# A gated block of linear attention and a bilinear feed-forward layer: the output projection of the attention done by seven half-size products

## The chip, the cores and the metric

The kernel runs on one core of one Trainium2 chip. The metric is the device time of one execution in microseconds (us), taken as the median of several runs. A profile is one more execution, with a trace of every engine: TensorE (PE; its weight loads are listed as PEld), VectorE (DVE), ScalarE (ACT), GpSimd (POOL) and SyncE (SP), which here only issues DMAs.

## What is computed

There are S = 2048 tokens of D = 512 features, H = 32 heads of 16, F = 1792 hidden features, all in float32:

```python
g = sigmoid((x * gate_w).sum(-1, keepdims=True))
# a: linear attention
q, k, v = split(x @ wqkv)                            # 32 heads of 16
phi = lambda t: where(t > 0, t + 1, exp(t)) + 1e-6
kv  = einsum("bhsd,bhse->bhde", phi(k), v)
z   = einsum("bhsd->bhd", phi(k))
o   = einsum("bhqd,bhde->bhqe", phi(q), kv) / (einsum("bhqd,bhd->bhq", phi(q), z)[..., None] + 1e-6)
a   = o @ wo
# b: bilinear feed-forward
b   = ((x @ w_gate) * (x @ w_up)) @ w_down
out = g * a + (1 - g) * b
```

The kernel folds kv and wo into one 512 x 512 matrix W' (each head's 16 x 16 block of kv times its 16 rows of wo). What it calls o is then phi(q) divided by its denominator, and a = o @ W'.

## The kernel before

**Precision.** Every float32 operand is split into a high and a low part that TensorE takes as fp32r (`split`: ACT or DVE copies the high part, DVE subtracts it). `mm3` makes one product of three matmuls: high x high, the stationary operand's high part x low, low x high. Nearly all matmuls have 512 columns.

**Phase 1** computes k = x @ wk tile by tile (PSUM tile `pk`), phi(k) and the sums `gt` = phi(k)^T x, and the gate: `gcol` holds g, `ocol` holds 1 - g, one column per tile of 128 tokens.

**Phase 2** goes over two pairs (halves of 1024 tokens) of 16 units each, so units 0 to 31. A unit makes 1024 tokens x 256 columns of two products at once by the 2x2 scheme (Strassen and Winograd): `product(i, ...)` is one of seven products of six matmuls, with the factors of the weights (`wch`, `wcl`, out of `wr`) and of x (`xa`, `xb`, `xc1`, `xc4`, `xc6`, high and low). The products go in the order 2, 3, 4, 1, 5, 6, 7 into the PSUM banks Y, X, R, S (`bY` and so on); ACT copies (`m`, `cross`) and DVE sums (`bR`, `t`, `bS`) between them put the result together. 14 units of a pair are feed-forward units ("f", one block of 128 hidden features), whose two results are multiplied into a hidden tile (`cross`, split to `hh`, `hl`). Two are query units ("q", one group of 16 heads, which is two blocks of 128 features); before, they stand behind the feed-forward blocks 5 and 9, at units 6, 11, 22 and 27.

**The order is written out by hand.** Every engine's list keeps the order of the program. Within a unit there are named places, in this sequence:

```
product 2, high, product 3, low, e, down(0), product 4, m, c, down(1), d,
product 1, t, product 5, down(2), s, down(3), product 6, r, product 7, end
```

`later(n, place, fn)` puts work at a place of unit n. `down(k)` takes the next k tiles off a list `jobs`; the table `shares` says how many at each of a unit's four `down` places. A job of two feed-forward blocks is one PSUM tile `pdn` of 128 tokens x 512 features, six matmuls; then ACT (the first time) or DVE adds it, scaled by `ocol`, to the accumulator `acc` of these tokens in SBUF.

**W'** is made early in phase 2: `kv_unit` (`pkv`), `kv_split` (DVE masks it to blocks of heads with `bmask` as `kvm`; `kvmh`, `kvml` are its parts), `wp_unit(b)` for b = 0 to 3 (PSUM tile `pw`, three matmuls, at places (3, e), (3, d), (4, e), (4, d)), split and parked in DRAM (`wpark`).

**Attention** (`attention`): `quad` makes phi(q) on ACT and DVE (`ex`, `phq`) as the query unit's results come; four `z_part` on ACT and loads through DRAM (`terms`, `zt`) make the denominators in the next two units; `recip` inverts them, `norm` loads them spread out (`rb`), `norm_high` and `norm_low` make o and split it into hidden tiles; `weights` loads W' back; `last` puts eight jobs for this group on the list `jobs`, six matmuls each, scaled by `gcol`. So o @ W' is done per group of heads, and the two groups meet in `acc`.

**Queues.** SyncE issues loads and stores in program order (`dma`), GpSimd issues the accumulating DMAs (`dma_add`) and the output of the first pair. Factors of the weights and of x are also summed by such DMAs: `w_load` loads three blocks, `w_add` adds five; `cb_load`, `x_add`, `cb_split` do it for the second pair's x, which `reload` brings back at the end of the first pair. The hidden tiles have NH = 5 buffers, `acc` has 8 of one tile.

**The end.** Behind the last product 7 come `down(2)`, `low1` (DVE makes the low half of the last hidden tile's second half), `down(1)`, `low0` and what is left of `jobs`.

Of the kernel before, what the change touches and what calls it, by code (L numbers as in the profile page):

```python
# [7 lines left out]
F32 = mybir.dt.float32  # L8
# [6 lines left out]
P = 128  # L15
S = 2048
D = 512
# [13 lines left out]
HB = 8  # L31
NH = 5

# [5 lines left out]

SLOT = {3: 0, 4: 1, 2: 2, 5: 3, 1: 4, 6: 5, 7: 6}  # L40


@with_exitstack
def gated_mix(ctx: ExitStack, tc, xt, xp, x, wqkv, wq, wq_add, wo, wgu, wgu_add, wdn, gate_w, out):
# [75 lines left out]
    zpark = dram.tile([KT * KT, P, P // KT], F32, name="zpark")  # L120
    wpark = [[dram.tile([P, D], F32, name=f"wpark{b}{v}") for v in "hl"] for b in range(KT)]


    order = []
    for f in range(NF):
        order.append(("f", f))
        if f in (5, 9):
            order.append(("q", f // 9))
    units = len(order)
    order = [(pair, *u) for pair in range(NPAIR) for u in order]  # L130

# [49 lines left out]
    with tc.tile_pool(name="p1", bufs=2, reuse_waits="tile") as p1:  # L181
# [168 lines left out]
        pin(nc.vector.reciprocal(gcol, gcol))  # L350
        pin(nc.vector.tensor_scalar(ocol, gcol, -1.0, 1.0, op0=ALU.mult, op1=ALU.add))


# [9 lines left out]
    def do(n, place):  # L363
        for fn in at.pop((n, place), []):
            fn()

    def down(k):
        for fn in jobs[:k]:
            fn()
        del jobs[:k]  # L370

    shares = {2: (0, 1, 1, 1), 6: (1, 0, 1, 0), 7: (1, 0, 1, 0), 10: (1, 1, 1, 2), 11: (1, 2, 1, 2),
              12: (1, 1, 1, 2), 15: (1, 1, 1, 2)}
    early = {units: (2, 4, 2, 2), units + 1: (2, 2, 1, 1)}

    def share(n):
        return early.get(n) or shares.get(n % units, (1, 1, 1, 1))  # L380

# [101 lines left out]
    def down_tiles():  # L483
        return [p2.tile([P, D], F32R, tag=f"d{v}", name=f"d{v}", bufs=NH + 1) for v in "hl"]


    att = {}

    def wp_load():
        att["wv"] = [p2.tile([P, D], F32, tag="acc", name="wv", bufs=8) for _ in range(KT)]  # L490
        att["wo"] = [p2.tile([P, D], F32, tag="ph", name="wo_sb", bufs=4) for _ in range(KT)]
        for k in range(KT):
            dma(att["wv"][k], wqkv[k * P:(k + 1) * P, 2 * D:3 * D])
        for k in range(KT):
            dma(att["wo"][k], wo[k * P:(k + 1) * P, :])

    def g_evac():
        att["g"] = [p2.tile([P, D], F32, tag="acc", name="gts", bufs=8) for _ in range(KT)]
# [48 lines left out]
    def wo_split(b):  # L547
        if b % 2 == 0:
            att.setdefault("woh", []).append(hidden())
        split(*[v[:, b % 2] for v in att["woh"][b // 2]], att["wo"][b])  # L550
# [13 lines left out]
    banks = ["dn", "dn"]  # L564
    left = {(p, i): NF // 2 + 1 for p in range(NPAIR) for i in range(TPP)}

    def down_jobs(pair, group, col):

        def job(i):
            t = pair * TPP + i  # L570
            c, sl = divmod(i, CH // P)
            sl = slice(sl * P, (sl + 1) * P)
            s = col[:, t:t + 1]
            first = (pair, i) not in acc
            if first:
                acc[pair, i] = p2.tile([P, D], F32, tag="acc", name="acc", bufs=8)
            else:
                left[pair, i] -= 1
            ends = not left[pair, i]

            step = D // 2 if ends and pair and i == TPP // 2 - 1 else D
            for o in range(0, D, step):
                cols = slice(o, o + step)
                banks.reverse()
                pd = psum.tile([P, D], F32, tag=banks[0], name="pdn", bufs=2)[:, 0:step]
                for j, ((hh, hl), w2) in enumerate(group() if callable(group) else group):
                    mm3(pd, (hh[:, c, sl], hl[:, c, sl]), [v[:, cols] for v in w2], j == 0, j == 1)
                a = acc[pair, i][:, cols]
# [8 lines left out]
        return [lambda i=i: job((i + TPP // 2) % TPP) for i in range(TPP)]  # L597


    def attention(pair, j, n):  # L600
        phs, group, wrow = {}, {}, {}
        den = {}
        turns = n + 5 == units

        terms = dram.tile([KT, 4 * HB, DH, P], F32, name=f"terms{pair}{j}")
        there = dram.tile([4 * HB, KT, P], F32, name=f"den{pair}{j}")

# [8 lines left out]
        def z_part(i):  # L616
            r, c = parts[i]
            b = 2 * j + r
            z = p2.tile([P, CH], F32, tag="z", name="zq", bufs=4)
            act(z, phs[r, c], AF.Identity, scale=zcol[:, b:b + 1], bias=ezcol[:, b:b + 1])  # L620
            dma(terms[:, HB * i:HB * (i + 1)].rearrange("c h e t -> (h e) c t"), z.rearrange("p (c t) -> p c t", c=KT))

        def z_load(e):

            den[e] = p2.tile([P, KT, P], F32, tag="z", name="zt", bufs=4)
            dma(den[e], terms[:, :, e * KT:(e + 1) * KT].rearrange("c h e t -> (c h) e t"))

# [8 lines left out]

        def recip():
            d = den["d"]
            pin(nc.vector.reciprocal(d, d))
            dma(there.rearrange("h c t -> c h t"), d)  # L640

        def norm(i):
            r, c = parts[i]
            if r not in group:
                group[r] = hidden()
            rb = p2.tile([P, CH], F32, tag="z", name="rb", bufs=4)
            one = there[HB * i:HB * (i + 1)].rearrange("h c t -> h (c t)")
            dma(rb, one[:, None, :].to_broadcast([HB, DH, CH]))
            den[i] = rb

        def norm_high(i):
# [4 lines left out]
        def norm_low(i):  # L656
            r, c = parts[i]
            hh, hl = group[r]
            tt(hl[:, c], den[i], hh[:, c].bitcast(F32), ALU.subtract)

        def weights():
            for r in range(2):
                wrow[r] = down_tiles()
                for src, part in zip(wpark[2 * j + r], wrow[r]):
                    dma(part.bitcast(F32), src)

        def last():

            where = len(jobs) if turns else 0
            jobs[where:where] = down_jobs(pair, lambda: [(group[r], wrow[r]) for r in range(2)], gcol)  # L670

# [8 lines left out]
        for i in range(4):  # L680
            later(n + 3, "e", lambda i=i: norm(i))
        for i, places in enumerate((((n + 3, "s"), (n + 3, "r")), ((n + 3, "end"), (n + 4, "e")),
                                    ((n + 4, "c"), (n + 4, "d")), ((n + 4, "t"), (n + 4, "s")))):
            for fn, (m, place) in zip((norm_high, norm_low), places):
                later(m, place, lambda i=i, fn=fn: fn(i))
        later(*((n + 5, "e") if turns else (n + 3, "c")), weights)
        later(n + 4, "end", last)
        return quad


# [22 lines left out]
    g_evac()  # L713
    for b, (n, place) in enumerate(((1, "e"), (1, "e"), (2, "d"), (2, "s"))):
        later(n, place, lambda b=b: wo_split(b))
    later(0, "s", kv_zeros)
    later(1, "c", kv_unit)
    later(2, "c", z_there)
    later(5, "c", z_sums)
    later(2, "e", kv_split)  # L720
    for b, (n, place) in enumerate(((3, "e"), (3, "d"), (4, "e"), (4, "d"))):
        later(n, place, lambda b=b: wp_unit(b))
    for n, (i, k) in enumerate((i, k) for i in (2, 3, 4, 1, 6, 7) for k in range(2)):
        later(n, "s", lambda i=i, k=k: cb_load(i, k))
# [17 lines left out]
    for n, (pair, kind, m) in enumerate(order):  # L742
        entry = {}
        if n == 6:

            banks[0] = "att"
# [10 lines left out]
        if kind == "f":  # L757
            if half is None:
                half = (hid, entry["d"])
            else:  # L760
                jobs += down_jobs(pair, (half, (hid, entry["d"])), ocol)
                half = None
# [57 lines left out]
```

## Time and profile before

| what | us |
|---|---|
| median of 3 runs | 603.16 (603.09 to 603.17) |
| the profiled execution | 603.08 |
| its span, first to last instruction | 601.4 |
| TensorE busy | 596.5 (99%) |
| DVE busy | 441.9 (73%) |
| ACT busy | 309.2 (51%) |
| POOL busy | 47.1 (8%) |

The granted TensorE clock is 1.000 in this execution. A row of a timeline or chain reads: start in us, duration, engine, operation or line, output <- inputs, partitions x elements, count, and in brackets the idle time ahead of it with what ended it. The duration of a matmul in these rows reaches into the next one's, since matmuls are pipelined; the distance between two starts is what one takes in a row of them.

### The profile page before, as it was taken

The page shows a single profiled execution, that of the slowest core. Times are in us where ns is not written, and L with a number is a line of the kernel's source. Part 1 is how long each engine was busy: PE and PEld are TensorE (multiplying, and loading weights), DVE is VectorE, ACT ScalarE, POOL GpSimd, SP SyncE. Part 2 cuts the span into 40 slices and gives each one's busy share as a digit, 9 for nine tenths or more (in the row PEclk, how much of TensorE's full clock was granted, in tenths as well). Part 3 has the DMA queues.
Part 4 walks back from the last instruction along what each step waited for, and adds up shares of the span by engine and source line. Part 5 has one row for each costly group of instructions (what it writes and reads, how often), then busy time and mean ns, then how long its engine had stood idle before and what let it go on. Part 6 is the DMA issues. An engine that isn't in the chain of part 4 may idle for free.

```text
span 601.4 us, 7610 instructions
## 1 busy us (share of the span) xinstructions
PE 596.5 (99%) x2682; PEld 492.1 (82%) x2682; DVE 441.9 (73%) x693; ACT 309.2 (51%) x534; POOL 47.1 (8%) x63
## 2 busy tenths in 40 slices
PE   9999999999999999999999999999999999999997
PEld 6888888888888888888888888888888888888886
DVE  6977896776787689666888866456677986668864
ACT  3855765586449545373444534654474454643300
POOL 0011100000111110100000020010000000000000
PEclk9999999999999999999999999999999999999999
DMA  8577948667868969658479535334386563553303
GB/s 291 182 195 136 288 94 276 153 189 193 219 175 203 275 156 269 135 126 209 105 223 350 155 138 134 89 87 90 70 192 171 150 168 67 130 146 81 102 1 141
DMA packets 51046, 98.54 MB, mean 164 GB/s; under 512 B 6576, under 2 KB 17584, under 8 KB 50992
## 3 DMA queue, kind: packets, MB, share of 16 engines
q1 hardware_dynamic: 43312, 69.22, 34.1%
q0 software_dynamic: 7408, 28.32, 26.1%
q10 hardware_dynamic: 288, 0.52, 0.3%
q8 instruction: 21, 0.34, 0.2%
q14 instruction: 17, 0.14, 0.1%
HBM read 82.31 MB, written 16.25 MB: 164 GB/s over the span
## 4 chain that ended last, share of the span: by engine, by line
PE 99%; DVE 0%; issue 0%
PE pdn L52 33%; PE bR L52 15%; PE bY L52 14%; PE bX L52 14%; PE pk L52 7%; PE bS L52 7%; PE gt L52 7%; PE warm L52 1%; PE pw L52 0%; PE pkv L52 0%; DVE acc L64 0%; DVE xc1h L108 0%
## 5 line engine op out<-in xcount | busy, mean ns | idle before, releaser
L52 PE MATMUL pdn<-dl,hh 128*128 128x512 f32 x290 | 112.4, 388 | 0.0
L52 PE MATMUL pdn<-dh,hl 128*128 128x512 f32 x290 | 112.4, 388 | 0.0
L52 PE MATMUL pdn<-dh,hh 128*128 128x512 f32 x290 | 112.4, 388 | 0.0
L64 DVE SCALAR_TENSOR_TENSOR acc<-pdn,ocol,acc 128x512 f32<-128x512 f32 (+1 forms) x97 | 71.2, 742 | 30.2 <-PE pdn L52 30.0
L58 ACT ACTIVATE hh<-cross 128x512 fp32r<-128x512 f32 x56 | 35.2, 628 | 89.6 <-DVE cross L61 89.6
L61 DVE TENSOR_TENSOR wcl<-wr,wch 128x512 fp32r<-128x512 f32 (+1 forms) x96 | 73.2, 771 | 0.0
L52 PEld LDWEIGHTS pdn<-dh,hh 128*128 128x128 f32 x290 | 54.5, 188 | 11.2
L52 PEld LDWEIGHTS pdn<-dl,hh 128*128 128x128 f32 x290 | 54.5, 188 | 11.2
L52 PEld LDWEIGHTS pdn<-dh,hl 128*128 128x128 f32 x290 | 54.5, 188 | 11.1
L58 ACT ACTIVATE wch<-wr 128x512 fp32r<-128x512 f32 (+1 forms) x96 | 60.1, 694 | 0.0
L52 PE MATMUL bX<-xbh,wch 128*128 128x512 f32 x128 | 49.8, 389 | 0.0
L52 PE MATMUL bX<-xbl,wch 128*128 128x512 f32 x128 | 49.8, 389 | 0.0
L52 PE MATMUL bX<-xbh,wcl 128*128 128x512 f32 x128 | 49.8, 389 | 0.0
L61 DVE TENSOR_TENSOR bR<-bX,m 128x512 f32<-128x512 f32 x32 | 22.3, 696 | 36.6 <-PE bX L52 31.7
L85 POOL DMA_DIRECT2D wr<-in_wgu_add x28 | 24.3, 868 | 309.5 <-ACT wr L58 175.2
L58 ACT ACTIVATE cross<-bY 128x512 f32<-128x512 f32 x32 | 19.1, 598 | 50.6 <-PE bY L52 50.2
L61 DVE TENSOR_TENSOR t<-bR,cross 128x512 f32<-128x512 f32 x32 | 22.1, 690 | 24.9 <-PE bR L52 11.5
L61 DVE TENSOR_TENSOR hl<-cross,hh 128x512 fp32r<-128x512 f32 x56 | 38.2, 683 | 0.8
L58 ACT ACTIVATE wr<-wr 128x512 f32<-128x512 f32 x64 | 36.5, 620 | 1.2 <-DMA wr<-in_wgu 1.2
L64 DVE SCALAR_TENSOR_TENSOR acc<-pdn,gcol,acc 128x512 f32<-128x512 f32 x32 | 23.7, 749 | 17.5 <-PE pdn L52 17.4
L58 ACT ACTIVATE cross<-bX 128x512 f32<-128x512 f32 x32 | 19.1, 597 | 32.8 <-DVE bS L61 32.6
L58 ACT ACTIVATE m<-bY 128x512 f32<-128x512 f32 x32 | 19.1, 597 | 22.4 <-PE bY L52 22.2
(158 smaller groups left out, 1256.6 us busy)
## 6 DMA issues: line engine op xcount, KB each, us to landing
wr<-in_wgu_add POOLq DMA_DIRECT2D x28, 640.0 KB, 6.3
wr<-in_wgu SPq DMA_DIRECT2D x28, 384.0 KB
wdr<-in_wdn SPq DMA_DIRECT2D x28, 256.0 KB
xraw<-in_x SPq DMA_DIRECT2D x16, 256.0 KB
terms<-zq SPq DMA_DIRECT2D x16, 256.0 KB
zt<-terms SPq DMA_DIRECT2D x16, 256.0 KB
rb<-den SPq DMA_DIRECT2D x16, 256.0 KB
xtraw<-in_xt SPq DMA_DIRECT2D x12, 256.0 KB
```

Source lines behind the costliest of these rows:

```text
L52: tc.keep_in_program_order(nc.tensor.matmul(*args, **kw))
L58: pin(nc.scalar.activation(dst, src, func, **kw))
L61: pin(nc.vector.tensor_tensor(dst, a, b, op=op))
L64: pin(nc.vector.scalar_tensor_tensor(dst, a, scalar, b, op0=op0, op1=op1))
L85: tc.keep_in_program_order(nc.gpsimd.dma_start(dst, src, accum_op=ALU.add))
```

## The change

o @ W' is now one product per pair over both groups of heads: o has 2 x 2 blocks (groups of heads by chunks of 512 tokens), W' has 2 x 2 blocks (halves of the 512 output features by groups of heads), and seven products of their sums replace eight block products.

- The gate g is multiplied into o: the column goes through DRAM (`gpark`) into the tile that held the mask, and `recip` multiplies the inverse by it. The store of the column stands right behind phase 1, ahead of phase 2's loads on SyncE.
- `norm_end` writes each block of o to DRAM (`opark`), and two negated ones.
- `wp_unit` now stands at (2, c), (2, d), (3, e), (3, c); ACT copies W' out, halves go to DRAM (`wraw`), `wp_minus` negates two blocks. From unit 4 on, `ow_load`, `ow_add`, `ow_split` sum and split the seven factors of W', one per unit.
- `o_products` adds 14 jobs per pair (seven products by halves of 512 tokens): in steps (four to a unit, at e, c, t, end) the factor of o is loaded, a step pair later summed by accumulating DMA, a step pair later split (`ready`) and put on a list of its own; `down` takes such a job behind its tiles. A job is 12 matmuls of 256 columns into the PSUM tile `po`, and one or two DVE sums of 512 elements per partition into `acc`. Two of the products go on in the bank of the one before. In all there are 336 such matmuls. The units with these jobs are 12 to 16 and 27 to 31.
- The query units stand behind blocks 2 and 5 in the first pair, behind 1 and 4 in the second: units 3, 7, 18 and 22. NH is 4, `acc` is 4 buffers of two tiles, and the table `shares` changes: unit 16 has (1, 1, 1, 2) instead of (2, 4, 2, 2), unit 17 has (1, 1, 1, 1) instead of (2, 2, 1, 1). `z_there`, `z_sums` and the second bank for down tiles (unit 4 instead of 6) come earlier.

```diff
-NH = 5
+NH = 4
+HALF = D // 2
+OPROD = (
+    (1, ("11", "22"), ("11", "22"), False, (("11", 1),)),
+    (6, ("-11", "21"), ("11", "12"), True, (("22", 1),)),
+    (5, ("11", "12"), ("-22",), False, (("12", -1),)),
+    (7, ("-22", "12"), ("21", "22"), True, (("11", 1),)),
+    (2, ("21", "22"), ("11",), False, (("21", 1), ("22", -1))),
+    (4, ("22",), ("-11", "21"), False, (("11", 1), ("21", 1))),
+    (3, ("11",), ("-22", "12"), False, (("12", 1), ("22", 1))),
+)
+STEPS = ("e", "c", "t", "end")
...
+    for pair, after in enumerate(((2, 5), (1, 4))):
+        for f in range(NF):
+            order.append((pair, "f", f))
+            if f in after:
+                order.append((pair, "q", after.index(f)))
...
+        dma(gpark.rearrange("t p -> p t"), gcol)
...
     def down(k):
         for fn in jobs[:k]:
             fn()
         del jobs[:k]
+        while ojobs and ojobs[0][0] < passed[0]:
+            ojobs.pop(0)[1]()
+        passed[0] += 1
...
-    shares = {2: (0, 1, 1, 1), 6: (1, 0, 1, 0), 7: (1, 0, 1, 0), 10: (1, 1, 1, 2), 11: (1, 2, 1, 2),
-              12: (1, 1, 1, 2), 15: (1, 1, 1, 2)}
-    early = {units: (2, 4, 2, 2), units + 1: (2, 2, 1, 1)}
+    shares = {2: (0, 1, 1, 1), 3: (1, 0, 1, 0), 4: (1, 0, 1, 0), 7: (1, 1, 0, 1), 8: (1, 1, 0, 1), 9: (1, 0, 1, 0)}
+    shares.update({units: (1, 1, 1, 2), units + 1: (1, 1, 1, 1)})
+    shares.update({units + m: v for m, v in ((2, (0, 1, 1, 1)), (3, (1, 0, 1, 0)), (4, (1, 0, 1, 0)),
+                                             (5, (1, 1, 0, 1)), (6, (1, 1, 0, 1)), (7, (1, 0, 1, 0)),
+                                             (15, (1, 1, 0, 1)))})
...
     def wp_unit(b):
+        j, r = divmod(b, 2)
         pw = psum.tile([P, D], F32, tag="att", name="pw", bufs=2)
-        mm3(pw, [v[:, b] for v in att["kvm"]], [v[:, b % 2] for v in att["woh"][b // 2]], True, True)
-        d = down_tiles()
-        split(*d, pw)
-        for there, part in zip(wpark[b], d):
+        mm3(pw, [v[:, b] for v in att["kvm"]], att.pop(("woh", b)), True, True)
+        att["w", b] = w = p2.tile([P, D], F32, tag="ph", name="wrow", bufs=4)
+        act(w, pw)
+        for m in range(2):
+            dma(wraw[f"{m + 1}{j + 1}"][:, r], w[:, m * HALF:(m + 1) * HALF])
+    def ow_split(p):
+        hi, lo = ws.pop(p)
+        act(hi, lo.bitcast(F32))
+        tt(lo, lo.bitcast(F32), hi.bitcast(F32), ALU.subtract)
+        for there, part in zip(wpark[p], (hi, lo)):
             dma(there, part.bitcast(F32))
...
         def recip():
             d = den["d"]
             pin(nc.vector.reciprocal(d, d))
-            dma(there.rearrange("h c t -> c h t"), d)
+            tt(d, d, bmask, ALU.mult)
+            for c in range(2):
+                dma(there[c].rearrange("h c t -> c h t"), d[c * P // 2:(c + 1) * P // 2])
...
+        def norm_end(i):
+            r, c = parts[i]
             stt(den[i], phs[r, c], EPS, den[i], ALU.add, ALU.mult)
-            act(group[r][0][:, c], den[i])
+            o_there(f"{j + 1}{c + 1}", r, den[i])
+            if j == c:
+                act(phs[r, c], den[i], scale=-1.0)
+                o_there(f"-{j + 1}{c + 1}", r, phs[r, c])
...
+    def o_products(pair, step0):
+        def ready(k, place):
+            tiles[k] = o_tiles()
+            split(*tiles[k], raw.pop(k).rearrange("p r t -> p (r t)"))
+            ojobs.append((passed[0] - (place == "end"), lambda: job(k)))
+        def job(k):
+            p, h = divmod(k, 2)
+            _, _, _, goes_on, sums = OPROD[p]
+            ot = [v.rearrange("p (r t) -> p r t", r=2) for v in tiles.pop(k)]
+            w2 = [v.rearrange("p (r c) -> p r c", r=2) for v in wt[p]]
+            if not goes_on:
+                banks.reverse()
+                bank[h] = psum.tile([P, 2, HALF], F32, tag=banks[0], name="po", bufs=2)
+            for s in range(2):
+                for r in range(2):
+                    mm3(bank[h][:, s], [v[:, r, s * P:(s + 1) * P] for v in ot], [v[:, r] for v in w2],
+                        not goes_on and s == r == 0, s == r == 1, True)
+            for block, sign in sums:
+                m, c = int(block[0]) - 1, int(block[1]) - 1
+                a = acc[pair, 2 * c + h][:, :, m * HALF:(m + 1) * HALF]
+                tt(a, a, bank[h], ALU.add if sign > 0 else ALU.subtract)
...
+    for b, (n, place) in enumerate(((2, "c"), (2, "d"), (3, "e"), (3, "c"))):
         later(n, place, lambda b=b: wp_unit(b))
...
-        if n == 6:
+        if n == 4:
             banks[0] = "att"
```

More of the change, by code (lines that the diff above doesn't have):

```diff
@@ L120, in gated_mix @@
     zpark = dram.tile([KT * KT, P, P // KT], F32, name="zpark")
-    wpark = [[dram.tile([P, D], F32, name=f"wpark{b}{v}") for v in "hl"] for b in range(KT)]
+    wraw = {b: dram.tile([P, 2, HALF], F32, name=f"wraw{b}") for b in ("11", "12", "21", "22", "-11", "-22")}
+    wpark = [[dram.tile([P, D], F32, name=f"wpark{i}{v}") for v in "hl"] for i in range(len(OPROD))]
+    gpark = dram.tile([NT, P], F32, name="gpark")
     order = []
[L125 to L130, printed above, removed]
+    for pair, after in enumerate(((2, 5), (1, 4))):
[3 more added lines that the diff above has]
+                order.append((pair, "q", after.index(f)))
+    units = len(order) // NPAIR
     raws, wcs = {}, {}
@@ L497, in g_evac @@
     def g_evac():
-        att["g"] = [p2.tile([P, D], F32, tag="acc", name="gts", bufs=8) for _ in range(KT)]
+        att["g"] = two_by_two("gts")
         for d in range(KT):
@@ L564, in gated_mix, with down_jobs @@
     banks = ["dn", "dn"]
-    left = {(p, i): NF // 2 + 1 for p in range(NPAIR) for i in range(TPP)}
-    def down_jobs(pair, group, col):
+    left = {(p, i): NF // 2 for p in range(NPAIR) for i in range(TPP)}
+    oleft = [2 * len(OPROD) for _ in range(NPAIR)]
+    def down_jobs(pair, group):
         def job(i):
@@ L572, in job @@
             sl = slice(sl * P, (sl + 1) * P)
[L573 to L578, printed above, removed]
+            s = ocol[:, t:t + 1]
+            if (pair, i // 2) not in acc:
+                acc[pair, i // 2] = p2.tile([P, 2, D], F32, tag="acc", name="acc", bufs=4)
+            first = left[pair, i] == NF // 2
+            left[pair, i] -= 1
             ends = not left[pair, i]
+            assert not ends or not oleft[pair]
             step = D // 2 if ends and pair and i == TPP // 2 - 1 else D
@@ L597, in down_jobs @@
         return [lambda i=i: job((i + TPP // 2) % TPP) for i in range(TPP)]
+    opark = {(p, b): dram.tile([2, P, 2, HALF], F32, name=f"opark{p}{b}") for p in range(NPAIR)
+             for b in ("11", "12", "21", "22", "-11", "-22")}
     def attention(pair, j, n):
[L601 to L606, printed above, removed]
+        phs, den = {}, {}
+        terms = dram.tile([2, KT, 2 * HB, DH, P], F32, name=f"terms{pair}{j}")
+        there = dram.tile([2, 2 * HB, KT, P], F32, name=f"den{pair}{j}")
         def quad(r, c, q):
@@ L681, in attention @@
             later(n + 3, "e", lambda i=i: norm(i))
[L682 to L687, printed above, removed]
-        return quad
+        for i, (m, place) in enumerate(((n + 3, "s"), (n + 3, "r"), (n + 3, "end"), (n + 4, "e"))):
+            later(m, place, lambda i=i: norm_end(i))
@@ L760, in gated_mix @@
             else:
-                jobs += down_jobs(pair, (half, (hid, entry["d"])), ocol)
+                jobs += down_jobs(pair, (half, (hid, entry["d"])))
                 half = None
```

106 lines of the change are left out of this document (75 added, 31 removed).

## The prediction

> **What bounds the kernel now.** I read the page first (busy time by engine, granted clock, the chain that ended last), then TensorE's timeline at the end of the run, then the chain in time around each place that the change touches. From the page of the kernel before:
>
> ```profile
> span 601.4 us, 7610 instructions
> ...
> PE 596.5 (99%) x2682; PEld 492.1 (82%) x2682; DVE 441.9 (73%) x693; ACT 309.2 (51%) x534; POOL 47.1 (8%) x63
> ...
> PEclk9999999999999999999999999999999999999999
> ...
> PE 99%; DVE 0%; issue 0%
> ```
>
> TensorE is busy for 99% of the span, at full clock in every slice, and the chain that ends last is TensorE's own list. So the time is the sum of its matmuls. A matmul less is worth its full spacing, and any new idle time of TensorE is paid in full. The other engines have room on average only, so each place where their order changes is looked at by itself. The profiled execution took 603.08 us, 1.68 more than its span; it lies 0.08 under the median of 603.16, so a difference added to either says the same. The three runs lie within 0.08, and I take 0.2% (1.2 us) as what a measurement tells from no change: "same" is 601.95 to 604.37.
>
> **1. The matmuls.** What o @ W' cost per group of heads was 8 tiles of 6 matmuls with 512 columns; two groups, two pairs: 192 matmuls. After, each pair has 14 jobs of 12 matmuls with 256 columns, together 336. The kernel before has both sizes back to back in its last tiles (columns: start, us, engine, line, operation):
>
> ```profile
> 587.66 0.39 PE L52 MATMUL pdn<-dl,hh 128*128 128x512 f32 x1
> ...
> 596.05 0.39 PE L52 MATMUL pdn<-dh,hl 128*128 128x512 f32 x1
> 596.28 0.28 PE L52 MATMUL pdn<-dh,hh 128*128 128x256 f32 x1
> 596.39 0.28 PE L52 MATMUL pdn<-dl,hh 128*128 128x256 f32 x1
> ...
> 597.59 0.28 PE L52 MATMUL pdn<-dh,hl 128*128 128x256 f32 x1
> ```
>
> The durations (0.39, 0.28) overlap, so I go by starts. From 587.66 to 596.05 there are 37 steps: 0.2267 us each. From 596.39 to 597.59 there are 10: 0.120 each. 192 x 0.2267 = 43.5 goes, 336 x 0.120 = 40.3 comes: **-3.2 us**. Seven products in place of eight should give an eighth, 5.4; the small matmul costs more than half of the large one (0.113), and that takes 2.2 back. The ends for this term are 0.110 (596.28 to 596.39) and 0.127 (0.120 plus the 0.007 by which it exceeds half): -6.5 to -0.8. I take 0.120, ten intervals in a row of the same kind.
>
> What of weight loads? Each matmul has one, and the profile shows the last ones thus:
>
> ```profile
> 597.35 0.19 PEld L52 LDWEIGHTS pdn<-dl,hh 128*128 128x128 f32 x1
> 597.47 0.19 PEld L52 LDWEIGHTS pdn<-dh,hl 128*128 128x128 f32 x1
> ```
>
> They start 0.12 apart too, and each lasts longer (0.19) than the matmul's own spacing, so they run under other matmuls. The Trainium skill ("TensorE: Matmul & The Clock Gate", The mechanism) says that a weight load overlaps matmuls in flight only where their row groups differ, which full 128-row tiles don't. By that rule load and matmul would add up; the 0.120 spacing in this trace contradicts it.
>
> **2. Unit 2: W' before its mask is ready.** Before, the first block of W' stood in unit 3, at 129.95 us. After, it stands in unit 2 right behind product 4, ahead of a down-projection tile. Its stationary operand is the masked k-v matrix. Chain in time, then DVE and ACT, before:
>
> ```profile
> 117.71 1.36 PE pdn L52 x6
> 129.95 0.68 PE pw L52 x3
> 118.26 0.85 DVE L61 TENSOR_TENSOR kvm<-pkv,bmask 64x256 f32<-64x256 f32 x2
> 119.21 0.63 ACT L58 ACTIVATE kvmh<-kvm 128x512 fp32r<-128x512 f32 x1 [2.49 <-DVE kvm L61]
> 119.87 0.69 DVE L61 TENSOR_TENSOR kvml<-kvm,kvmh 128x512 fp32r<-128x512 f32 x1 [0.76 <-ACT kvmh L58]
> ```
>
> Product 4 ends at 117.71, where the tile begins; there TensorE now wants the matrix. Its high part is ready at 119.84, its low part at 120.56. DVE's and ACT's lists up to there are unchanged. The first two of the three matmuls of a block use the high part, the third the low part. The high part alone costs 119.84 - 117.71 = 2.1 and up to a weight load (0.19) more; the third matmul, due at 117.71 + 0.45, can start at 120.56 to 120.75: 2.4 to 2.6. With some room for the hand-over of a semaphore 2.2 to 2.8, I take **+2.5**. Nothing can fill this hole, since TensorE's list is fixed; the tile that covered it comes behind.
>
> **3. Unit 16, the start of the second pair.** Before, four tiles stood between product 4 and product 1; after, one.
>
> ```profile
> 332.60 5.44 PE pdn L52 x24
> 338.04 1.36 PE bR L52 x6
> 332.70 0.60 ACT L58 ACTIVATE cross<-bY 128x512 f32<-128x512 f32 x1 [3.80 <-PE bY L52]
> 333.19 1.05 ACT L58 ACTIVATE xc1h<-xc1l 128x1024 fp32r<-128x1024 f32 x1
> 334.27 1.22 DVE L61 TENSOR_TENSOR xc1l<-xc1l,xc1h 128x1024 fp32r<-128x1024 f32 x1 [2.24 <-ACT xc1h L58]
> ```
>
> ACT makes the operand of product 1 only after copying product 4 out, and DVE ends its low part at 335.49. Product 1 used to start at 338.04, 2.5 later. With one tile of 1.36 it could start at 333.96 and needs the low part a matmul later, 334.19: about 1.3 missing, plus a weight load: **+1.35**, bounds 1.0 and 1.6.
>
> **4. The tail.** Before, attention tiles lay behind the last product 7 and gave DVE time for the low half of the last hidden block. After, they are gone, and two tiles are left.
>
> ```profile
> 576.04 21.84 PE pdn L52 x102
> 578.80 0.75 DVE L64 SCALAR_TENSOR_TENSOR acc<-pdn,gcol,acc 128x512 f32<-128x512 f32 x1 [0.61 <-PE pdn L52]
> 579.46 0.68 DVE L61 TENSOR_TENSOR hl<-cross,hh 128x512 fp32r<-128x512 f32 x1
> ```
>
> The low half is ready at 580.14. The sixth matmul of the third tile needs it at 576.04 + 2 x 1.36 + 5 x 0.2267 = 579.89; with the load **+0.45** (0.2 to 0.6).
>
> **5. Units 3 and 4: queries earlier.** The first group of heads moves from unit 6 to unit 3, where ACT also copies two blocks of W' and negates quarters of them, and the first sums start. Around the old place:
>
> ```profile
> 188.19 0.62 ACT L58 ACTIVATE phq<-bS 128x512 f32<-128x512 f32 x1
> 193.01 0.62 ACT L58 ACTIVATE cross<-bY 128x512 f32<-128x512 f32 x1
> 193.97 0.69 DVE L61 TENSOR_TENSOR t<-bR,cross 128x512 f32<-128x512 f32 x1 [1.51 <-ACT cross L58]
> 196.60 1.36 PE bR L52 x6
> L58 ACT ACTIVATE dh<-pw 128x512 fp32r<-128x512 f32 x4 | 2.4, 600 | 1.3 <-PE pw L52 0.9 <-ACT dh L58 0.4
> ```
>
> ACT is behind after the query unit; that delays the copy of product 4 and so `t`, which ends at 194.66, 1.94 ahead of product 6. Two copies of W' add 1.2, with the negations (an estimate: half of 0.6 each, for half the columns, and a fixed part) about 2.2. Against 1.94 that is 0 to 1.0 lost; I take **+0.3**, as most of the copies fall early in unit 3.
>
> **6. What I cost at nothing, and its cover.** VectorE in the units with o products:
>
> ```profile
> L64 DVE SCALAR_TENSOR_TENSOR acc<-pdn,ocol,acc 128x512 f32<-128x512 f32 x95 | 70.3, 747 | 30.0 <-PE pdn L52 29.8
> L61 DVE TENSOR_TENSOR bR<-bX,m 128x512 f32<-128x512 f32 x32 | 22.3, 696 | 36.6 <-PE bX L52 31.7 <-ACT m L58 4.7
> 225.00:240.00 15.00, 15.00 (x68) 12.43 (x67) 13.59 (x22) 7.54 (x14) 0.87 (x1) 1.00 0.91 270
> ```
>
> The worst unit has 11 operations of its own, 4 splits of o and 8 sums, all like the second row (23 x 0.696 = 16.0), and 4 tiles (3.0): 19.0. Its matmuls take 42 + 24 of 0.2267 and 48 of 0.120: 20.7. That is 92%; in the window before (span 15; PE, PEld, DVE, ACT busy) VectorE ran at 13.59 of 15, 91%, while TensorE stood never. Without that margin each per cent costs 0.2 per such unit, with six of them.
>
> Queues: SyncE gets the writes of o, the loads of its blocks and of the seven factors; GpSimd the accumulating DMAs. A block is loaded two steps ahead of its accumulation and that two steps ahead of its split, and there are four steps to a unit of about 20 us, so 9 us for either.
>
> ```profile
> cbs<-in_xp POOLq DMA_DIRECT2D x10, 256.0 KB, 6.1
> 87.55 0.38 SPq L82 DMA_DIRECT2D zpark<-zacc  x1
> 87.98 0.91 SPq L82 DMA_DIRECT2D wdr<-in_wdn  x1
> 90.36 0.25 DVE L350 RECIPROCAL gcol<-gcol 128x16 f32<-128x16 f32 x1
> 94.24 0.62 ACT L58 ACTIVATE dh<-wdr 128x512 fp32r<-128x512 f32 x1
> ```
>
> 6.1 us from issue to landing for this size fits into that; 3 remain. The store of the gate column, 2048 pieces of 4 bytes, stands ahead of the first weight load on SyncE and waits for the reciprocal: it is issued at 90.6, done issuing by about 91.0, so the load comes 3 us later than 87.98. It is wanted at 94.24, so its transfer has 3.2 us; cover without reserve, cost 0 to 2.
>
> Sum: -3.2 + 2.5 + 1.35 + 0.45 + 0.3 = +1.4, on 603.08 or 603.16 **604.6 us**. With the ends of all terms it lies between 603.08 - 6.5 + 3.4 = 600.0 and 603.08 - 0.8 + 6.0 + 2 = 610.3, corners that need all ends at once.
>
> **Rivals.** *Not slower:* the seven products give what their number says. If 256 columns cost half of 512, 0.1134, the first term is 43.5 - 38.1 = -5.4, and the sum 602.4. For it: the one interval of 0.110; against: the ten of 0.120. It is within "same" as soon as a small matmul costs under 0.1194 (-3.4), with the other terms as above, and "faster" needs the waits at their lower ends as well (-5.4 + 3.4: 601.1). The Trainium skill (same page, Back-to-back issue gap) gives N / 2.4 + 2.5 ns, which would be 109 and 216 ns: 4.8 less by its figures and 603.0 in the sum; this trace shows 120 and 227. Waits smaller than I worked out end there too: chance 0.2 together.
>
> *The clock:* the hole of 2.5 us in unit 2 drops TensorE's clock for a while. The trace shows what cold matmuls cost, at the start:
>
> ```profile
> L52 PE MATMUL warm<-xc1h 128*128 128x512 bf16 x8 | 3.6, 631 | 1.3 <-DVE xc1h L108 1.3
> ```
>
> Eight take 3.6 us, where eight at 0.2267 take 1.8: one such stretch again costs 1.8, so 606.4. Against it: the hole is short, and the granted clock was full throughout. The Trainium skill (same page, Why this matters for your kernels) asks for no idle gaps over about 3 us; no run here shows a gap of that length. Chance 0.07.
>
> *Transfers or VectorE late:* an o block lands after its split is due, or the gate column's 4-byte pieces hold the queue. The split waits at the head of ACT's or VectorE's list and the products' evacuations behind it. It decides as soon as a 256 KB accumulation takes over 9 us in a unit, beside a DMA share already at 0.91 in the window above. Half a us in each of six units: 3 more, 607.6. Chance 0.17.
>
> *Loads bind:* if loads of 0.19 don't overlap, the 336 take 336 x (0.19 + 0.120) = 104.2 in place of 40.3: 668. Against it the spacing of 0.12. Chance 0.01.
>
> **The numbers.** The forecast has 0.55, its own range 603.4 to 606.2 (ends of terms 2 to 5, and 0.118 to 0.122 per small matmul). The range 602.0 to 608.0 leaves out about half of the "not slower" case and what of the late transfers exceeds 3.4 us. Same: half of the "not slower" case and a quarter of the forecast, 0.25; faster 0.1; slower 0.65.
>
> **What would show it.** In the profile after: a group of `po` matmuls with 256 columns that start 0.120 apart; idle time of TensorE ahead of `pw` released by ACT `kvmh` and DVE `kvml` near 118 to 121 us; ahead of `bR` in unit 16, released by `xc1`; ahead of `pdn` in the tail, released by `hl`; full clock. I'm wrong if `po` starts lie closer than 0.118, if TensorE doesn't wait in unit 2, or if it waits in the units with o products.

## The result, and the profile after

The changed kernel takes 644.74 us, the median of 4 runs (643.93 to 645.91), against 603.12 before (4 runs, 602.95 to 603.17): ratio 1.0692, 95% interval 1.0674 to 1.0711. It is 41.6 us slower, where 1.4 were forecast and the range ended at 608. The profiled execution took 645.20, with a span of 643.4.

The page of the changed kernel:

```profile
span 643.4 us, 8244 instructions
...
PE 607.4 (94%) x2826; PEld 500.3 (78%) x2826; DVE 455.2 (71%) x720; ACT 323.9 (50%) x565; POOL 68.5 (11%) x88
...
PEclk9999997999999989979999999999999999999999
...
PE 78%; DMA 12%; DVE 4%; ACT 3%; issue 2%; SPq 0%; DVEq 0%; POOLq 0%; ACTq 0%
```

TensorE is no longer the whole chain. DMA has 12% of it, and the granted clock has dents that the kernel before had not, all before the middle. The waits say where (engine, line, waited for: us in total, times, longest). TensorE's:

```profile
PE bR L68 <- DVE t L77: 17.5, 3, 9.1
PE bY L68 <- ACT m L74: 7.3, 3, 6.1
PE pw L68 <- ACT kvmh L74: 2.2, 1, 2.2
```

`t` and `m` are the ordinary links of a unit. They are late because their engines stand at something else, which ACT's and DVE's waits name:

```profile
ACT owh L74 <- DMA owl<-wraw: 14.0, 4, 6.0
...
ACT dh L74 <- DMA wdr<-in_wdn: 10.2, 1, 10.2
...
DVE rb L80 <- DMA rb<-den: 10.9, 3, 6.1
```

These are the splits of W' factors, the first down weights, and the denominators of both groups of heads (the longest wait, 6.1 us, is the second group's): three kinds of DMA.

For a sum by place I use one measure. For every matmul I take the step to the next start, less its regular step (0.2267 for 512 columns and 0.120 for 256, both worked out in the prediction); what is over is idle time or a slow matmul. I call it the excess, added up by unit. Span less excess is then the sum of the regular steps, with the time ahead of the first matmul (1.3 us) and behind the start of the last one (3.8 us):

| kernel | span | start | units 0-1 | 2-3 | 4 | 5-11 | 12-15 | 16-17 | 31 | all | span less excess |
|---|---|---|---|---|---|---|---|---|---|---|---|
| before | 601.4 | 2.1 | 0.2 | 0 | 0 | 0 | 0 | 0 | 0 | 2.2 | 599.2 |
| after | 643.4 | 2.0 | 12.3 | 2.8 | 2.3 | 25.3 | 0.2 | 1.6 | 0.7 | 47.4 | 596.0 |

The last column falls by 3.2 us, but that follows from the number of matmuls and the steps that the measure takes as given. That the step of 0.120 holds in the changed kernel is seen in units 12 to 15: they have 156 of the 336 small matmuls, and an excess of 0.2 us. Units 0-1 and 5-11 hold 37.6 of the 47.4 us of excess, and of these the prediction had nearly nothing. The second pair, with the same seven products, has no hole in units 18 to 30.

The first place, in the chain in time (start, us, what) and in SyncE's timeline:

```profile
91.07 13.35 DMA wdr<-in_wdn
...
108.16 2.92 PE bR L68 x6
```

```profile
90.57 0.38 SPq L98 DMA_DIRECT2D gpark<-gcol  x1
91.07 0.81 SPq L98 DMA_DIRECT2D wdr<-in_wdn  x1
91.92 2.16 SPq L98 DMA_DIRECT2D wv<-in_wqkv  x4
94.19 10.62 SPq L98 DMA_DIRECT2D wo_sb<-in_wo  x4
```

The load of the first down weights, right behind the store of the gate column, needs 13.35 us. And the four issues of `wo_sb` take 10.62, where they took 1.75 before, so the queue takes next to nothing in that time. The row of the kernel before:

```profile
91.78 1.75 SPq L82 DMA_DIRECT2D wo_sb<-in_wo  x4
```

The six matmuls after the hole take 2.92 instead of 1.36. The DMA share falls meanwhile. The row of the kernel before, from the issue of the same load on, and two of the changed kernel (window, span, busy time of PE, PEld, DVE, ACT, POOL, clock, DMA share, GB/s):

```profile
88.00:91.00 3.00, 3.00 (x15) 2.49 (x14) 2.65 (x8) 0.22 (x1) 0.00 (x0) 1.00 0.91 184
```

```profile
91.00:94.00 3.00, 3.00 (x15) 2.49 (x14) 1.03 (x2) 1.48 (x3) 0.00 (x0) 1.00 0.31 3
94.00:97.00 3.00, 3.00 (x15) 2.49 (x14) 0.70 (x1) 0.26 (x1) 0.00 (x0) 1.00 0.09 21
```

So the DMA engines are not busy with the small pieces; the loads stand behind them. The second place, in the chain around unit 7:

```profile
202.61 12.62 DMA owl<-wraw
...
215.73 6.68 DMA owl<-wraw
222.44 0.64 ACT owh L74
```

A factor's load lands 12.6 us after its issue, then its accumulation takes 6.7, and TensorE stands for 7.2 us ahead of product 6.

### The profile page after: what moved, and what is told of

The parts are those of the page before. It is cut to its first block, busy times and chain, and to the rows that moved or that the text cites. A ratio compares the mean times of both kernels' runs of the same rounds, so it can differ in the third digit from the quotient of the medians.

```text
span 643.4 us, 8244 instructions
## 1 busy us (share of the span) xinstructions
PE 607.4 (94%) x2826; PEld 500.3 (78%) x2826; DVE 455.2 (71%) x720; ACT 323.9 (50%) x565; POOL 68.5 (11%) x88
## 4 chain that ended last, share of the span: by engine, by line
PE 78%; DMA 12%; DVE 4%; ACT 3%; issue 2%; SPq 0%; DVEq 0%; POOLq 0%; ACTq 0%
PE pdn L68 19%; PE bR L68 11%; PE bY L68 11%; PE bX L68 10%; DMA owl<-wraw 8%; PE pk L68 7%; PE gt L68 7%; PE po L68 6%; PE bS L68 6%; DMA wdr<-in_wdn 2%; DMA rb<-den 2%; DMA owl<-wraw-11_100 1%; DVE acc L80 1%; ACT wch L74 1%; PE warm L68 1%
## 5 line engine op out<-in xcount | busy, mean ns | idle before, releaser
L68 PE MATMUL pdn<-dh,hl 128*128 128x512 f32 (+1 forms) x226 | 88.1, 390 | 0.3 <-DVE hl L77 0.3
L68 PE MATMUL pdn<-dh,hh 128*128 128x512 f32 (+1 forms) x226 | 88.1, 390 | 0.0
L68 PE MATMUL pdn<-dl,hh 128*128 128x512 f32 (+1 forms) x226 | 88.1, 390 | 0.0
L68 PEld LDWEIGHTS pdn<-dh,hl 128*128 128x128 f32 x226 | 42.7, 189 | 9.6 <-DVE hl L77 0.7
L68 PEld LDWEIGHTS pdn<-dl,hh 128*128 128x128 f32 x226 | 42.7, 189 | 8.6
L68 PEld LDWEIGHTS pdn<-dh,hh 128*128 128x128 f32 x226 | 42.7, 189 | 8.6
L68 PE MATMUL bR<-xc6h,wch 128*128 128x512 f32 x64 | 26.6, 416 | 17.5 <-DVE t L77 17.5
L77 DVE TENSOR_TENSOR acc<-acc,po 128x512 f32<-128x512 f32 x40 | 26.4, 685 | 11.1 <-PE po L68 10.8
```

The costliest lines, as they stand in the source:

```text
L68: tc.keep_in_program_order(nc.tensor.matmul(*args, **kw))
L77: pin(nc.vector.tensor_tensor(dst, a, b, op=op))
```

## The experiments

Two theories were to be told apart for each place: at unit 0 the small pieces or the place in the queue; in units 5 to 11 the W' chain by itself or DMA engines that are full. Excess by place, from the profile of each run, in the order below:

| kernel | time | units 0-1 | 2-3 | 4 | 5-11 | 12-15 | 16-17 | all |
|---|---|---|---|---|---|---|---|---|
| after | 644.74 | 12.3 | 2.8 | 2.3 | 25.3 | 0.2 | 1.6 | 47.4 |
| e1 gate in few pieces | 635.74 | 0.8 | 4.3 | 2.3 | 23.7 | 2.1 | 1.6 | 38.1 |
| e2 gate behind loads | 640.84 | 3.4 | 4.9 | 2.3 | 25.9 | 2.0 | 1.6 | 43.2 |
| e8 before, with gate store | 612.69 | 9.9 | 0 | 0 | 0 | 0 | 0 | 11.9 |
| e10 before, spaced pieces | 604.53 | 1.5 | 0 | 0 | 0 | 0 | 0 | 3.7 |
| e3 split later | 648.05 | 11.4 | 4.4 | 2.3 | 25.7 | 1.3 | 1.7 | 50.4 |
| e4 no factor DMAs | 623.90 | 0.8 | 4.0 | 2.3 | 12.7 | 1.9 | 1.6 | 26.2 |
| e5 no x DMAs | 626.47 | 0.8 | 4.4 | 2.3 | 15.7 | 0.2 | 1.7 | 28.6 |
| e6 neither | 609.18 | 0.7 | 4.0 | 2.2 | 0 | 0.2 | 1.6 | 11.5 |
| e11 norm spread | 637.50 | 0.8 | 4.2 | 2.3 | 26.6 | 1.6 | 1.6 | 40.0 |
| e7 two waits covered | 633.32 | 0.8 | 0 | 2.3 | 23.9 | 1.8 | 4.0 | 35.7 |
| e9 all waits away | 609.64 | 0.8 | 0 | 2.2 | 3.8 | 0.2 | 1.7 | 11.9 |
| e13 minus earlier | 611.45 | 0.9 | 4.5 | 2.6 | 0 | 0.2 | 1.6 | 13.7 |
| e12 cheap edits together | 632.41 | 0.8 | 0.1 | 2.0 | 27.6 | 0.2 | 1.7 | 35.6 |

The times of the first and the last row are medians of 4 runs, the others single runs; the kernel before took 602.92 to 604.01 beside them. The four runs of e12 lie 4.8 us apart, so I read less than that between two single runs of the changed kernel from the places in the profile, not from the time.

### The gate store: e1, e2, e8, e10

```diff
...
-        dma(gpark.rearrange("t p -> p t"), gcol)
+        pin(nc.vector.transpose(gturn, gsq))          # gcol is gsq[:, 0:NT]
+        for j in range(KT):
+            dma(gpark[:, j * P // KT:(j + 1) * P // KT], gturn[j * P // KT:j * P // KT + NT])
```

> The changed kernel with the gate column turned by VectorE's 32 x 32 transpose first, so that it goes to DRAM in four stores of 16 rows x 128 bytes instead of one of 2048 pieces of 4 bytes; its place on SyncE's list stays. Theory (the small pieces stall the queue behind them): the first wdr load, which landed 13.4 us after its issue, lands within 4 us as before, TensorE's hole of 9.3 us in unit 0 and the slow matmuls behind it go, 11.8 us less: about 633 us. Rival (the place ahead of the loads is what costs): the hole stays above 5 us, 640 or more.

635.74; the excess of units 0-1 falls from 12.3 to 0.8. The place in the list is as before, so it is the pieces. The time falls by 9.0 only and ends 2.7 above the forecast, since units 2-3 and 12-15 now lose 3.4 more.

```diff
     d_load(1)
+    dma(gpark.rearrange("t p -> p t"), gcol)         # and not behind phase 1
```

> The changed kernel with the same store of 2048 pieces of 4 bytes moved behind phase 2's first loads (two of wdr, four of wv, four of wo) on SyncE. If only the place matters, unit 0's hole goes and nothing comes for it: about 633 us. If the pieces hold the queue for some 10 us wherever they stand, the hole goes from unit 0 and the loads next in the queue are late (the second unit's factors or x blocks): between 636 and 645, with a new wait in unit 1 or 2.

640.84, in the middle of what was expected: the hole moves to unit 1, 3.2 us, where ACT waits for the factors of unit 2:

```profile
ACT wch L74 <- DMA wr<-in_wgu_add: 8.9, 1, 8.9
```

The pieces cost something in both places; how much depends on what comes next.

The store alone, added to the kernel before:

> The kernel before, with nothing but the store of the gate column to DRAM added (2048 pieces of 4 bytes, at the changed kernel's place, read by nobody). Theory: the first wdr load lands some 9 us late, ACT waits for it and TensorE behind ACT, with slow matmuls after the hole: 9 to 12 us more, 612 to 615. Rival (the store alone is hidden; it takes the other loads of the changed kernel): within 2 us of the kernel before.

612.69, 9.5 more than the 603.21 beside it, all of it in unit 0.

```diff
-    gpark = dram.tile([NT, P], F32, name="gpark")
+    gpark = dram.tile([NT, P, 32], F32, name="gpark")
...
-        dma(gpark.rearrange("t p -> p t"), gcol)
+        dma(gpark[:, :, 0].rearrange("t p -> p t"), gcol)
```

> The kernel before with the added store of the gate column as in the run with that store, but each piece of 4 bytes goes into a slot of its own of 128 bytes. If neighbouring pieces that share a line of memory hold the queue, the hole of unit 0 goes: under 605. If any piece of 4 bytes does, it stays: 611 to 614.

604.53: as many pieces, of the same 4 bytes, from the same place, and 1.1 us of hole. So neither the number of the pieces nor their size is enough to hold the queue; it is held when they lie side by side in memory. Why neighbours do that, no run here shows.

### Units 5 to 11: e3, e4, e5, e6, e11

```diff
-        later(5 + p, "c", lambda p=p: ow_split(p))
+        later(5 + p, "r", lambda p=p: ow_split(p))
```

> The changed kernel with each split of a factor of W' moved from place c to place r of the same unit, about 9 us later; loads and accumulations stay. Theory (the split waits for its accumulating DMA at the head of ACT's list, and the evacuations and splits of the unit behind it): most of the waits of units 5 to 10 go, and what of unit 11 came from that lag: 15 to 25 us less, 620 to 630. Rival (the queues are full, and the later split only moves the wait): less than 8 us gained.

648.05, no gain. ACT no longer waits for the factors, but the holes are as large; it now waits for others (`wr`, `cbs`) and DVE for `rb`. The rival has it: the wait only moves. My theory, a split set too early, falls. The next two runs take transfers away. Of the chain of W' (with e1's gate):

```diff
     def ow_load(p):
         ws[p] = ow_tiles()
-        dma(ws[p][1].bitcast(F32), wraw[OPROD[p][1][0]].rearrange("p r c -> p (r c)"))
+        pin(nc.gpsimd.memset(ws[p][1].bitcast(F32), 0.0))
...
-        later(4 + p, "s", lambda p=p: ow_add(p))
```

> Gate column as in the kernel with the transpose, and the factors of W' neither loaded nor accumulated: a memset by GpSimd fills the tile, the splits and their stores stay (so the products use zeros for W'). Theory: without these transfers ACT never waits for them, units 5 to 11 run without holes, and what is left of the excess is units 2, 4, 16 and the tail, some 7 us, minus the 3.2 saved: 606 to 610. Rival (the blocks of o, their stores and the denominators' loads are late by themselves in the first pair): a hole of over 4 us stays in unit 7 or 11, 615 or more.

And of the second pair's x (`cb_load` becomes a memset, `x_add` keeps only its negation, `cb_split` stores nothing, and `reload` brings nothing or one unsummed block):

> Gate column as in the kernel with the transpose, chain of W' factors unchanged, but the transfers that make the second pair's factors of x during the first pair are left out (loads, accumulations and stores of cbs; the second pair then computes with stale and unsummed factors). The work of ACT and VectorE on them stays. Theory (the 16 DMA engines are full from unit 4 to unit 11, and each chain is late because the engines are): with some 4 us of transfers less in each of these units the holes of units 5 to 11 go, though the W' chain and its places are as before: 24 us of excess there become under 5, 612 to 618. Rival (the W' chain's three transfers one behind another in one unit are too slow by themselves): the holes stay, 630 or more.

623.90 and 626.47, with 12.7 and 15.7 of the 23.7 us left in units 5 to 11. Each expectation named one cause. The first result is on the rival's side (a hole of 4.6 us stays in unit 11), the second lies between the two. The hole in unit 11 isn't behind a factor of W': there the chain runs over the denominators of the second group of heads, in e4 and in the changed kernel alike.

```profile
248.62 10.27 DMA rb<-den
```

```profile
265.61 10.17 DMA rb<-den
```

Both taken away:

> As the last, and the loads and accumulations of the factors of W' left out too (zeros instead). Theory: no hole over 0.5 us is left in units 5 to 11; the excess is unit 2 (4), unit 4 (2), unit 16 (1.6), the tail (0.6) and the two or so of the start that the kernel before has as well: 608 to 611. Rival (the blocks of o come late for another reason than full DMA engines, such as the order on SyncE's list): a hole of 3 us or more stays in unit 7 or 11, 613 or more.

609.18, as forecast, and no hole in units 5 to 15. The windows of these stretches show what the engines carried. Before, after, and without W' transfers, without x transfers, without both:

```profile
150.00:300.00 150.00, 150.00 (x663) 124.23 (x662) 113.75 (x174) 78.64 (x139) 16.55 (x19) 1.00 0.73 188
```

```profile
150.00:300.00 150.00, 131.47 (x541) 103.95 (x540) 98.62 (x157) 80.58 (x144) 21.45 (x25) 0.95 0.93 249
```

```profile
150.00:300.00 150.00, 140.57 (x617) 113.19 (x617) 109.40 (x170) 81.91 (x146) 22.05 (x28) 0.99 0.93 257
```

```profile
150.00:300.00 150.00, 139.08 (x599) 112.69 (x598) 107.41 (x169) 78.94 (x140) 19.78 (x26) 0.97 0.79 217
```

```profile
150.00:300.00 150.00, 149.36 (x685) 123.92 (x684) 118.60 (x184) 86.02 (x153) 21.04 (x30) 1.00 0.78 218
```

The last two columns are DMA share and GB/s, the third is TensorE's busy time. The kernel before ran this stretch at 0.73 with TensorE full. After, the DMA engines are at 0.93 while TensorE stands for 18.5 us: they are as good as full. Without the W' transfers the share stays 0.93, as the kernel gets through more of its units in that time (617 matmuls instead of 541). The kernel of e1, from which these three runs differ, has 0.93 and 255 GB/s there too. Without the x transfers it drops to 0.79 and an excess remains, of 4.1 and 8.1 us in units 5 and 7, where ACT still waits for a factor's accumulation, and 2.5 in unit 11, behind the denominators. So the x transfers are worth 8 us when they alone are taken away, those of W' 11, and both together all 23.7. The sum of the transfers is thus shown as a cause. That the chain of three in one unit is one by itself is not: e4 takes away the chain and its bytes at once, and only the waits that stay in e5, at a share of 0.79, speak for it. In each place a transfer lands later than its place allows. The second pair has the same loads of denominators and makes no factors of W' or x; its share is 0.75 from 420 to 560 us, and it has no hole there.

Whether a burst ahead of a factor matters:

```diff
-        for i in range(4):
-            later(n + 3, "e", lambda i=i: norm(i))
+        for i, place in enumerate(("e", "c", "t", "s")):
+            later(n + 3, place, lambda i=i: norm(i))
```

> Gate column as in the kernel with the transpose; the four loads of the spread denominators (rb, 1 MB together), which stood at place e one behind another, are spread over the places e, c, t and s, so that a factor of W' is loaded ahead of three of them. Theory (the hole of unit 7 comes from the factor's load standing behind a burst of 1 MB on SyncE's queue): the 10 us there shrink by half, 628 to 632. Rival (only the sum of the transfers counts): within 2 us of 635.7.

637.50, no gain: unit 7 loses 6.5 instead of 10.4, but units 9 and 11 together 15.7 instead of 7.5. The rival holds: the waits only move.

### The small waits: e7, e9, e13, and e12

```diff
-    for b, (n, place) in enumerate(((2, "c"), (2, "d"), (3, "e"), (3, "c"))):
+    for b, (n, place) in enumerate(((2, "t"), (2, "s"), (3, "e"), (3, "c"))):
         later(n, place, lambda b=b: wp_unit(b))
...
-    shares.update({units: (1, 1, 1, 2), units + 1: (1, 1, 1, 1)})
+    shares.update({units: (1, 3, 1, 0), units + 1: (1, 1, 1, 1)})
```

> Gate column as in the kernel with the transpose; the first two blocks of W' go from (2, c) and (2, d) to (2, t) and (2, s), behind a tile and product 1, and unit 16 has the shares (1, 3, 1, 0), three tiles between product 4 and product 1. Theory for these two places: the holes of 2.3 us and 1.0 us there and the slow matmuls behind the first go, about 5.5 us of excess. If the DMA engines set the pace of units 5 to 11, what is gained ahead of them in unit 2 is mostly lost again there: 632 to 634.5; if these holes add up with the others: 630.

633.32, in the interval of the first case. Unit 2's excess goes from 4.3 to 0. Unit 16's doesn't: with three tiles ahead of product 1 its hole goes, but with none behind `s`, product 7 waits twice for the split of its own factor of x (0.9 us for the high part, 1.0 for the low part), with slow matmuls after it: 4.0 in units 16-17 instead of 1.6.

> As the kernel without transfers for x and for the factors of W' (zeros and stale factors), and the other waits covered as well: the first two blocks of W' at (2, t) and (2, s), unit 16 with the shares (1, 2, 1, 1), and the copies and negations of the blocks of W' on VectorE instead of ScalarE. Theory (the sum is closed: with every wait named so far taken away only the saving on the matmuls is left): 609.2 less 4.0 for unit 2, 1.5 for unit 16 and 2 for unit 4, 601 to 602, under the kernel before; the 336 small matmuls take 40.3 us. Rival (ScalarE's lag in unit 4 has another cause than the copies, or the copies only delay VectorE): unit 4 keeps its 2 us, 603 to 604.

609.64, outside both cases. Unit 2 is clean, but units 5 to 11 have 3.8, in unit 8 behind a load of weights and in unit 11 behind the denominators, and 16-17 still 1.7. My reading is that what TensorE gains early it waits for later, even with this traffic; no run separates it from the work that moved to VectorE. Unit 4 keeps 2.2, so it isn't who copies W'. In e6's profile ACT has this wait there:

```profile
ACT phq L74 <- DMA wraw-22_94<-wrow: 2.0, 1, 2.0
```

The last phi(q) tile takes over the buffer of a block of W' whose negated copy is still being stored.

```diff
-    for b, (n, place) in enumerate(((2, "end"), (3, "e"), (3, "t"), (3, "s"))):
+    for b, (n, place) in enumerate(((2, "end"), (3, "e"), (3, "c"), (3, "d"))):
         later(n, place, lambda b=b: wp_minus(b))
```

> As the kernel without transfers for x and for the factors of W' (zeros and stale factors), with the negations of the third and fourth block of W' moved from (3, t) and (3, s) to (3, c) and (3, d), still on ScalarE. Theory (the last phi(q) tile of unit 3 waits for the buffer that the last negated block is being stored from): its wait of 2 us goes, unit 4 keeps only the 0.66 at its start, 609.2 - 1.6 = 607.6. Rival (ScalarE's list is too long there): unit 4 keeps 2 us or unit 3 gets as much, 609 or more.

611.45, on the rival's side; unit 4 has 2.6. (About 1.2 of the 2.3 us more than e6 lie ahead of unit 0, which no edit touched.) That wait is gone, but the negation, which works in place, now waits for the store of the plain block:

```profile
ACT wrow L74 <- DMA wraw<-wrow: 1.5, 1, 1.5
```

ACT has no idle time from there to unit 4, so a wait of either kind comes out at TensorE. Which of the two, buffer or list, would suffice alone isn't settled.

The edits that leave nothing out, together (e1's gate, W' at (2, t) and (2, s) with copies and negations on VectorE, unit 16 with (1, 2, 1, 1), spread denominators):

> Nothing left out: gate column by the transpose, first blocks of W' at (2, t) and (2, s), unit 16 with (1, 2, 1, 1), copies and negations of W' on VectorE, loads of the denominators spread. What these edits can reach while the DMA engines are full in units 4 to 11: 622 to 631, still slower than the kernel before. If the holes were independent of one another it would be 635.7 - 4.3 - 1.5 - 2.2 - 5 = 622 to 623.

632.41 (4 runs, 628.87 to 633.62), ratio 1.0459 (1.0424 to 1.0495), just above the expected 622 to 631. The holes are not independent: unit 2's 4 us are gone, and units 5 to 11 have 27.6. None of these versions beats the kernel before, not even e9, which leaves out the transfers of x and W'. A version that does would have to take transfers out of units 4 to 11 without leaving work out, the sums of W' made in SBUF for one, and cover the small waits too; that wasn't tried.

## Why the prediction was wrong, by its steps

**1, the matmuls: right.** A job of the changed kernel, in the chain:

```profile
308.36 1.43 PE po L68 x12
```

1.43 / 12 = 0.119. From each start to the next, all 336 take 40.1 us, where 40.3 were forecast. The rival that a small matmul costs half, and the one of weight loads, fall.

**2, unit 2: right.** 2.34 of hole for 2.2 to 2.8, waiting for `kvmh` as said; a wait for `kvml`, which was named too, isn't listed.

**3 and 4, unit 16 and the tail: right in kind, small.** 1.63 for 1.35, 0.66 for 0.45. In unit 16 0.44 of it is a wait for the high part of the factor, which I had left out, and 1.03 the wait for the low part.

**5, units 3 and 4: mis-sized, 2.3 for 0.3.** I counted ACT's operations against a slack of 1.94; what came on top was an idle time of ACT of 2.0, in e6 named as a wait for a store out of a reused buffer, which no step of mine had.

**6, the edits costed at nothing: here it failed.** Two sentences did it. "Cover without reserve, cost 0 to 2" for the gate store: the bound was taken from the issue time and the room for one load, as if 2048 pieces of 4 bytes were like the 2048 of `zpark` ahead of it. They cost 9.5 alone, and 12.3 of excess here, where 0 to 2 were allowed. And "6.1 us from issue to landing for this size fits into that; 3 remain": I took the landing from a median over the kernel before and compared it with the chain of o, which did keep its time: units 12 to 15 have 0.2 us of excess, and VectorE's cover of 92% there was enough. The chain of W', with load, accumulation and split inside the length of one unit, some 14 us, and two stores behind, I never priced, nor the loads of the denominators at their new place, and I never added the new megabytes to a DMA share that I had quoted at 0.91 for a window of that very stretch. What the sum had at nothing was 25.3.

**The rivals.** "Transfers late" had a chance of 0.17 and a price of 3 us. Of its two conditions the gate column's pieces came true; an o block landing late did not, and the factors of W' and the denominators, which it didn't name, did. Its price was at fault too: half a us a unit was a guess, where the profile's DMA share said how little was free. The forecast's own range is off as a sum: the ends that it names give 602.6 to 606.6, not 603.4 to 606.2; against 644.7 that decides nothing. "The clock" did not come true at the place that it named in the changed kernel, but in e1 it did. Windows from unit 2's hole of 2.3 us on, in e1 and in the changed kernel (the last three columns are the granted clock, DMA share and GB/s):

```profile
118.00:121.00 3.00, 0.82 (x4) 0.39 (x3) 2.23 (x5) 0.98 (x2) 0.00 (x0) 1.00 0.73 238
121.00:123.00 2.00, 2.00 (x6) 1.29 (x6) 0.98 (x2) 1.26 (x3) 0.00 (x0) 0.65 0.47 173
123.00:125.00 2.00, 2.00 (x6) 1.51 (x6) 0.00 (x0) 0.31 (x1) 0.00 (x0) 0.50 0.67 235
```

```profile
129.00:132.00 3.00, 0.82 (x5) 0.35 (x3) 2.23 (x6) 0.76 (x2) 0.00 (x0) 1.00 0.73 212
132.00:134.00 2.00, 2.00 (x8) 1.36 (x9) 1.19 (x2) 1.48 (x3) 0.00 (x0) 1.00 0.63 243
```

The same hole, followed by half the clock in one and full clock in the other; it costs 2.0 us in slow matmuls or 0.4. Seven more runs have this hole of 2.3 us, and slow matmuls of 1.7 to 2.5 us behind it. The longer holes of units 0, 7 and 11 of the changed kernel are all followed by slow matmuls, 2.4 to 2.8 us of excess each, about 8 of its 47.4. The Trainium skill's limit of about 3 us of idle time ("TensorE: Matmul & The Clock Gate", Why this matters for your kernels) is a little too kind here: 2.3 us can do it.

## What to carry to other kernels

When a change turns on-chip work into transfers, add their time on the DMA engines to the share that the stretch already has, unit by unit, before pricing any single landing; at 0.93 the loads of a W' factor here landed after 3.9 to 12.6 us, so a median landing time of another kernel said little. A chain of load, accumulation and split is best given its own line in the sum, with the queue that each step stands in. And where one hole is covered, look whether the next transfer was waiting for the same moment: here part of several gains came back as waits some units later (e1, e7, e12).

## What the runs showed that was not expected

2048 pieces of 4 bytes written side by side hold SyncE's queue for about 10 us (they add 9.5 us to the kernel before, e8), though their own time on the engines is short: in the changed kernel all of them have begun by 93 us, at some 7 ns each, and at 91 to 97 us the DMA share is 0.31 and 0.09. The same pieces in slots of 128 bytes cost 1.2 (e10, 604.53 against the 603.29 beside it), and turned on VectorE into 64 rows of 128 bytes they leave 0.6 us of excess in unit 0 (e1).
